# Third layer of an attention and two-MLP kernel: weight conversion pipelined over blocks, adding transfers in groups of six, first product block by block

## The chip, the cores and the metric

One NeuronCore of a Trainium2 chip runs the whole program. The metric is the device time of one execution in microseconds (us); of three runs of the kernel before, the median is 631.76 us (631.39 to 633.15). A change of under about 0.3% (1.9 us) can't be told from none.

The engines are TensorE (PE, with its weight loads PEld), VectorE (DVE), ScalarE (ACT) and GpSimd (POOL). Each works through its own queue in order, and so does SyncE (SP), which issues most transfers. POOL issues the transfers that add.

## The reference, cut to what matters

```
attn_out = attention(q, k, v)          # 2 batches, 8 heads, 768 x 64, banded mask
x = attn_out as 1536 x 512
a, b = x @ moe_w1, x @ moe_w2          # first MLP, d_ff 1024
x = ((a * b) @ moe_w3) @ moe_w_out
a, b = x @ moe2_w_a, x @ moe2_w_b      # second MLP, d_ff 1536
out = (a * b) @ moe2_w_out             # 1536 x 1536 times 1536 x 512: the third layer below
```

The weights are float64 and reach the chip as pairs of 32-bit words; q, k, v and the result are float32.

## The kernel before, in words

The change lies in the last 150 us: in the end of `products` and in `output`. Three things have to be known.

**Weights.** A block of 128 rows of `moe2_w_out` (blocks f = 0 to 11) is loaded as raw words by `wo_load` (L1013, queue SP) and turned into float32 by `convert`: ACT takes the two words apart (L89, L90), DVE joins them in three steps (L94, L98, L102) into the tile `wof`, ACT rounds the value to a high part (L115), and DVE subtracts to get the low part (L119); both parts are the tile `wo2`, which the trace shows as `wo_band`. `wo_steps(f)` does this for one block from first to last step; `fill` lets it advance between the products of PE.

**Products.** Every product of high and low parts is three matmuls (`multiply`, L931). `output` has two stages. The first is a plain product for the last 512 rows of the output: twelve blocks f of 12 matmuls 128x512, three into each of four PSUM banks. For each pair of blocks the left side is split into its parts by `rest_steps` (ACT L1028, DVE L1030). After block 11, ACT copies the four banks out (L1209).

The second stage computes the other 1024 rows with seven products of half-size matrices in place of eight, in the order 1, 2, 7, 6, 4, 5, 3. Each product is 72 matmuls 128x256 into four banks (rows i = 0 to 3), over six blocks f. The generator `prepare` makes the operands; one of its stages is run (`next(turns)`) ahead of each product, so what it puts into the queues of ACT and DVE stands ahead of that product's own evictions (ACT L1240, DVE L1243). An operand of the left side is made by `left`: a cast on ACT (L733), a subtraction on DVE (L734). There are eight PSUM banks: products 1 and 2 fill four each, and product 7 takes over the four of product 2 when DVE has evicted them (L1243).

**Adding transfers.** `add` (L1126) is a transfer issued from POOL that adds one 128x512 tile to another in SBUF. There are four sums for each f = 0 to 5, called S1 to S4 here: S1 is `ga[f][:,0] += ga[f][:,1]`, S2 `ga[f][:,1] += ga[f+6][:,1]`, S3 `ga[f][:,0] += ga[f+6][:,1]`, S4 `ga[f+6][:,0] += ga[f][:,0]`. S1 may start when the operand of product 1 for this f has been made (`first_left`), since it overwrites its source; S2 has to wait for S1 of the same f, which reads what S2 writes. Product 7 reads the sums S1, product 6 S3, product 5 S2 and product 3 S4.

The order of the work is that in which the Python code emits it; each engine's queue keeps that order, and an engine waits at an instruction whose semaphore has not come.

Of the kernel before, what the change touches and what calls it, by code (L numbers as in the profile page):

```python
# [9 lines left out]
F32R = mybir.dt.float32r  # L10
# [6 lines left out]
P = 128  # L17
# [14 lines left out]
class Emitter:  # L32
# [981 lines left out]

    def wo_steps(self, f):
        if f % 2 == 0:
            self.wo_whole[f // 2] = self.unit("wof", [P, 2, self.DM])
        t = self.unit("wo2", [P, 2, 1, self.DM], F32R)
        g = self.wo_whole[f // 2][:, f % 2 : f % 2 + 1]
        for stage in self.convert(t[:, 0], t[:, 1], self.wo_raw.pop(f), g):  # L1020
            for _ in stage():
                yield
        self.wo[f] = t

# [14 lines left out]
    def products(self, ops, tail):  # L1039


        nc, C, nf2 = self.nc, self.C, self.NF2
        H = TG // 2
# [3 lines left out]
        self.ga, self.gb = ga, gb  # L1047
        self.wo_raw, self.wo, self.wo_whole, self.rests = {}, {}, {}, {}
        order0 = [(0, 1), (0, 7), (0, 2), (0, 6), (0, 4), (1, 1), (1, 7), (0, 5), (1, 6), (1, 4), (1, 2), (1, 5), (0, 3), (1, 3)]
        order = [(0, 1), (0, 7), (1, 1), (1, 7), (0, 6), (0, 4), (1, 6), (1, 4), (0, 5), (1, 5), (0, 2), (1, 2), (0, 3), (1, 3)]  # L1050
# [4 lines left out]
        for f in range(nf2):  # L1055
# [10 lines left out]
            for slot, (q, k) in enumerate(order if f else order0):  # L1066
# [5 lines left out]
                if f == nf2 - 1:  # L1072
                    if slot in (0, 2, 4):
                        self.wo_load(slot // 2)
                    if slot == 2:
                        steps += [self.wo_steps(0), self.rest_steps(0), self.wo_steps(1), self.wo_steps(2)]
                    if slot > 2:
                        self.fill(steps)
                for _ in range(1 if f else 0 if slot < 3 else 1 if slot < 8 else 2):
# [39 lines left out]
    def output(self):  # L1119
# [34 lines left out]
        def first_left(f):  # L1154
            left(1, f, ga[f][:, 0])
            add(ga[f][:, 0], ga[f][:, 1])
            add(ga[f][:, 1], ga[f + K][:, 1])

        def prepare():
            lefts(2, lambda f: ga[f + K][:, 0])  # L1160
            for j in range(K // 2):
                b, d = whole[j], whole[j + K // 2]
                t3 = self.half("t3", [P, 2, H])
                sub(t3, d[:, :, high], b[:, :, high])
                right(7, t3)
            yield
            lefts(7, lambda f: ga[f][:, 0], lambda f: add(ga[f][:, 0], ga[f + K][:, 1]))
            for j in range(K // 2):
                b, d = whole[j], whole[j + K // 2]
                sub(b[:, :, low], b[:, :, high], b[:, :, low])  # L1170
                sub(b[:, :, high], d[:, :, high], b[:, :, low])
            yield
            for j in range(K // 2):
                right(6, whole[j][:, :, high], -1.0)
            lefts(6, lambda f: ga[f][:, 0], lambda f: add(ga[f + K][:, 0], ga[f][:, 0]))
            yield
            for j in range(K // 2):
                b, d = whole[j], whole[j + K // 2]
                sub(d[:, :, low], d[:, :, low], b[:, :, high])
                right(4, d[:, :, low], -1.0)  # L1180
            lefts(4, lambda f: ga[f + K][:, 1])
            yield
            for j in range(K // 2):
                right(5, whole[j][:, :, low], -1.0)
            lefts(5, lambda f: ga[f][:, 1])
            yield
            lefts(3, lambda f: ga[f + K][:, 0])
            yield
            yield

        banks = [self.bank("o") for _ in range(4)]
        for f in range(nf2):
            if f + 3 < nf2:
                self.wo_load(f + 3)
            steps = []
            if f + 3 < nf2:
                steps.append(self.wo_steps(f + 3))
            if f % 2 == 0 and f + 2 < nf2:
                steps.append(self.rest_steps(f // 2 + 1))
            hi, lo = self.rests[f // 2]  # L1200
            for n, p in enumerate(banks):
                at = slice(n * P, (n + 1) * P)
                left_part = hi[:, f % 2, at], lo[:, f % 2, at]
                self.multiply(p, [left_part], [(wo[f][:, 0, 0], wo[f][:, 1, 0])], f == 0, f == nf2 - 1)
                for _ in range(3):
                    self.fill(steps)
# [5 lines left out]
            for step in steps:  # L1212
                for _ in step:
                    pass
            for e in {8: (0,), 9: (1, 2), 10: (3, 4), 11: (5,)}.get(f, ()):
                first_left(e)
# [7 lines left out]
        turns = prepare()  # L1224
        z, x, m = [None] * 4, [None] * 4, [None] * 4
        sums = {}
        for k in (1, 2, 7, 6, 4, 5, 3):
            next(turns)
            for i in range(4):
                if k in (1, 2, 7):  # L1230
                    {1: z, 2: x, 7: m}[k][i] = self.bank("o", (P, H))
                bank = {2: x, 7: m, 4: m}.get(k, z)[i]
                h, e = divmod(i, 2)
                at = slice(i * P, (i + 1) * P)
                terms = [(t[:, 0, at], t[:, 1, at]) for t in la[k]]
                self.multiply(bank, terms, rb[k], k in (1, 2, 7), True, k in (6, 4, 5, 3))
                if k in (1, 7, 6, 3) and e == 0:
# [140 lines left out]
```

## Time and profile before

| | |
|---|---|
| median of 3 runs | 631.76 us |
| profiled execution: device time, span | 631.91 us, 630.0 us |
| TensorE busy | 588.9 us, 93% |
| VectorE, ScalarE, GpSimd busy | 452.5 us, 364.3 us, 156.2 us |
| granted clock, mean | 0.98 |
| first matmul of `output` | 500.09 us |
| first matmul of product 7 | 579.92 us |

Busy time of TensorE over the whole span hides where it waits: up to 500 us it is busy nearly without a break, and its idle time after that lies in the two stages of `output`. Times in the rows below are us from the start of the span, so they are to be compared with the 630.0 us and not with the 631.91 us.

### The profile page before, as it was taken

How to read it: one execution, taken by the hardware profiler on the slowest of the kernel's cores; microseconds unless marked ns; L12 is line 12 of the kernel's file. 1: busy time of each engine (PE TensorE's matmuls, PEld its weight loads, DVE VectorE, ACT ScalarE, POOL GpSimd, SP SyncE). 2: the span in 40 equal slices, each digit the busy share in tenths (PEclk: the TensorE clock that was granted, in tenths of full speed). 3: DMA queues.
4: the chain of work that ended last, by engine and by line, in shares of the span. 5: the costliest groups of instructions: out<-in, count | busy, mean ns of one | idle time of the engine just before them, and what ended most of it. 6: DMA issues, size and time to landing. Idle time of an engine off the chain costs nothing.

```text
span 630.0 us, 10247 instructions
## 1 busy us (share of the span) xinstructions
PE 588.9 (93%) x3632; PEld 511.6 (81%) x3632; DVE 452.5 (72%) x978; ACT 364.3 (58%) x796; POOL 156.2 (25%) x214
## 2 busy tenths in 40 slices
PE   6998999999999999999999999999999978881996
PEld 4677978888888888888999888888888856781996
DVE  6888899369774855489996777777776877645680
ACT  6998899656473746387544444454444555732450
POOL 5655766200000003216120222222222000136200
PEclk9999999999999999999999999999999988995999
DMA  8999762344242325967131221201221630457911
GB/s 239 268 254 211 194 175 71 137 135 164 89 170 74 133 68 105 227 137 107 27 134 34 68 82 56 80 17 68 68 67 63 206 100 33 111 92 130 172 48 59
DMA packets 28556, 73.63 MB, mean 117 GB/s; under 512 B 3408, under 2 KB 8016, under 8 KB 28496
## 3 DMA queue, kind: packets, MB, share of 16 engines
q1 hardware_dynamic: 20560, 57.42, 30.7%
q0 software_dynamic: 7360, 14.68, 13.6%
q10 hardware_dynamic: 576, 0.79, 0.5%
q8 instruction: 30, 0.49, 0.3%
q14 instruction: 30, 0.25, 0.1%
HBM read 55.05 MB, written 3.15 MB: 92 GB/s over the span
## 4 chain that ended last, share of the span: by engine, by line
PE 74%; DVE 11%; DMA 6%; ACT 5%; issue 3%; POOL 1%; POOLq 0%; DVEq 0%; ACTq 0%
PE ab_band L931 26%; PE y_band L931 9%; PE o_band L931 7%; PE ab_band L669 6%; PE ab_band L670 6%; PE ab_band L671 6%; DMA ga_band<-ga_band 4%; PE wfp_band L245 2%; PE wfp_band L244 2%; PE wfp_band L243 2%; PE pv_band L516 2%; PE pt_band L480 2%; DVE s_band L444 1%; DVE wof_band L102 1%; DVE wof_band L98 1%
## 5 line engine op out<-in xcount | busy, mean ns | idle before, releaser
L931 PE MATMUL ab_band<-y_band,ws_band 128*128 128x512 f32 (+1 forms) x576 | 110.2, 337 | 0.0
L931 PEld LDWEIGHTS ab_band<-y_band,ws_band 128*128 128x128 f32 x576 | 90.9, 190 | 12.2 <-ACT u_band L1085 0.2
L669 PE MATMUL ab_band<-xh_band,w_band 128*128 128x512 f32 (+1 forms) x216 | 81.8, 379 | 0.0
L671 PE MATMUL ab_band<-xh_band,w_band 128*128 128x512 f32 (+1 forms) x216 | 79.0, 366 | 0.0
L670 PE MATMUL ab_band<-xl_band,w_band 128*128 128x512 f32 (+1 forms) x216 | 79.0, 366 | 0.0
L931 PE MATMUL o_band<-wo_band,gs_band 128*128 128x256 f32 (+1 forms) x360 | 63.9, 339 | 9.2 <-DVE gs_band L1030 9.1
L469 POOL TENSOR_SCALAR s_band<-s_band,z_band 128x256 f32<-128x256 f32 (+1 forms) x96 | 61.1, 649 | 35.8 <-DVE z_band L467 15.5
L931 PEld LDWEIGHTS o_band<-wo_band,gs_band 128*128 128x128 f32 x360 | 55.1, 197 | 18.0 <-DVE gs_band L1030 11.2
L931 PE MATMUL y_band<-gs_band,wf_band 128*128 128x512 f32 (+1 forms) x336 | 58.4, 336 | 0.0
L931 PEld LDWEIGHTS y_band<-gs_band,wf_band 128*128 128x128 f32 x336 | 51.8, 190 | 6.6
L931 PE MATMUL ab_band<-y_band,wa_band 128*128 128x512 f32 (+1 forms) x288 | 56.4, 338 | 0.0
L90 ACT ACTIVATE raw_band<-raw_band 128x512 int32<-128x512 uint32 x76 | 51.1, 673 | 0.0
L931 PE MATMUL o_band<-wt_band,gs_band 128*128 128x256 f32 x288 | 36.7, 292 | 15.4 <-DVE s_band L1243 15.4
L931 PEld LDWEIGHTS ab_band<-y_band,wa_band 128*128 128x128 f32 x288 | 46.0, 190 | 6.1
L678 DVE TENSOR_TENSOR g_band<-ab_band,b_band 128x512 f32<-128x512 f32 (+1 forms) x27 | 16.9, 629 | 45.2 <-ACT b_band L677 45.2
L931 PEld LDWEIGHTS o_band<-wt_band,gs_band 128*128 128x128 f32 x288 | 36.5, 202 | 15.6 <-issue 15.6
L456 ACT ACTIVATE s_band<-s_band,m_band 128x256 f32<-128x256 f32 (+1 forms) x96 | 47.0, 499 | 3.5 <-DVE m_band L444 3.4
L669 PEld LDWEIGHTS ab_band<-xh_band,w_band 128*128 128x128 f32 x216 | 40.7, 188 | 7.5 <-issue 1.0
L671 PEld LDWEIGHTS ab_band<-xh_band,w_band 128*128 128x128 f32 x216 | 40.6, 188 | 6.7
L670 PEld LDWEIGHTS ab_band<-xl_band,w_band 128*128 128x128 f32 x216 | 40.7, 189 | 6.2
L1085 ACT COPY p_band<-ab_band 128x512 f32<-128x512 f32 (+1 forms) x48 | 21.9, 482 | 36.8 <-PE ab_band L931 36.8
L1126 POOL DMA_DIRECT2D ga_band<-ga_band x24 | 20.9, 1273 | 85.8 <-DVE gs_band L734 59.3
(149 smaller groups left out, 1205.3 us busy)
## 6 DMA issues: line engine op xcount, KB each, us to landing
raw_band<-in_moe_w_dram SPq DMA_DIRECT2D x31, 512.0 KB, 4.7
raw_band<-in_moe_w_out_dram SPq DMA_DIRECT2D x20, 512.0 KB, 3.6
raw_band<-in_moe_w_b_dram SPq DMA_DIRECT2D x12, 512.0 KB, 3.5
raw_band<-in_moe_w_a_dram SPq DMA_DIRECT2D x12, 512.0 KB, 4.4
ga_band<-ga_band POOLq DMA_DIRECT2D x24, 256.0 KB, 5.5
v_band<-in_v_dram SPq DMA_DIRECT2D x12, 256.0 KB, 8.1
kd_band<-in_kq_dram SPq DMA_DIRECT2D x12, 256.0 KB, 7.9
qd_band<-in_kq_dram SPq DMA_DIRECT2D x12, 256.0 KB, 7.9
```

What stands on the lines that cost most here:

```text
L90: nc.scalar.activation(out=low, in_=low.bitcast(U32), func=AF.Copy, scale=2.0**-29)
L243: nc.tensor.matmul(acc, w[:, 1, k % 4, :], o[:, 0, 0, :], start=(k == 0), stop=False)
L244: nc.tensor.matmul(acc, w[:, 0, k % 4, :], o[:, 1, 0, :], start=False, stop=False)
L456: nc.scalar.activation(out=s[:, j, lo:], in_=s[:, j, lo:], func=AF.Exp, bias=m[:, j : j + 1], scale=-1.0, accum_out=z[:, j : j + 1],)
L469: nc.gpsimd.tensor_scalar(out=s[:, j, lo:], in0=s[:, j, lo:], scalar1=z[:, j : j + 1], scalar2=1.0, op0=ALU.mult, op1=ALU.mult)
L669: nc.tensor.matmul(p, wl, xh, start=(c == 0), stop=False)
L670: nc.tensor.matmul(p, wh, xl, start=False, stop=False)
L671: nc.tensor.matmul(p, wh, xh, start=False, stop=(c == self.C - 1))
L678: nc.vector.tensor_tensor(out=out[:, at], in0=ps[0], in1=b, op=ALU.mult)
L931: self.nc.tensor.matmul(bank, wt, xt, start=start and i == n == 0, stop=stop and n == 2 and i == len(terms) - 1, skip_group_check=more,)
L1085: copy = lambda out: nc.scalar.copy(out=out, in_=bank)
L1126: add = lambda out, a: nc.gpsimd.dma_start(out, a, accum_op=ALU.add)
```

## The change

`wo_steps` becomes one generator over all twelve blocks: while block f is joined and rounded, block f+1 has been taken apart, and the low part of block f-1 is subtracted after the rounding of f. In the last block of `products` four raw blocks are loaded in place of three, and nine steps of the new generator are run; in `output`, `wo_until` runs it as far as a block needs, with a lead of three blocks, and blocks are loaded five ahead in place of three. `first_left` issues S1 only; f = 0 to 3 are emitted in the first stage, 4 and 5 in `prepare`. The sums S2 follow as a group behind the sums S3, and the sums S4 as a group behind the six operands of product 6. Product 1 runs block by block over its four banks in place of bank by bank.

```diff
-    def wo_steps(self, f):
...
+    def wo_steps(self):
+        stages = {}
+
+        def begin(f):
+            if f % 2 == 0:
+                self.wo_whole[f // 2] = self.unit("wof", [P, 2, self.DM])
+            g = self.wo_whole[f // 2][:, f % 2 : f % 2 + 1]
+            self.wo[f] = t = self.unit("wo2", [P, 2, 1, self.DM], F32R)
+            stages[f] = self.convert(t[:, 0], t[:, 1], self.wo_raw.pop(f), g)
+            for _ in stages[f].pop(0)():
+                pass
+
+        begin(0)
+        yield
+        for f in range(self.NF2 + 1):
+            if f + 1 < self.NF2:
+                begin(f + 1)
+            if f < self.NF2:
+                for stage in stages[f][:2]:
+                    for _ in stage():
+                        yield
+            if f:
+                for _ in stages.pop(f - 1)[2]():
+                    pass
+                self.wo_done = f
                 yield
-        self.wo[f] = t
+
+    def wo_until(self, f):
+        while self.wo_done < f:
+            next(self.wo_turns)
...
+        self.wo_done, self.wo_turns = 0, self.wo_steps()
...
-                    if slot in (0, 2, 4):
+                    if slot in (0, 2, 4, 6):
                         self.wo_load(slot // 2)
-                    if slot == 2:
-                        steps += [self.wo_steps(0), self.rest_steps(0), self.wo_steps(1), self.wo_steps(2)]
-                    if slot > 2:
-                        self.fill(steps)
+                    if slot == 5:
+                        steps.append(self.rest_steps(0))
+                    if slot > 4:
+                        next(self.wo_turns)
...
             add(ga[f][:, 0], ga[f][:, 1])
-            add(ga[f][:, 1], ga[f + K][:, 1])
 
         def prepare():
+            for f in (4, 5):
+                first_left(f)
             lefts(2, lambda f: ga[f + K][:, 0])
...
             lefts(7, lambda f: ga[f][:, 0], lambda f: add(ga[f][:, 0], ga[f + K][:, 1]))
+            for f in range(K):
+                add(ga[f][:, 1], ga[f + K][:, 1])
...
-            lefts(6, lambda f: ga[f][:, 0], lambda f: add(ga[f + K][:, 0], ga[f][:, 0]))
+            lefts(6, lambda f: ga[f][:, 0])
+            for f in range(K):
+                add(ga[f + K][:, 0], ga[f][:, 0])
...
+            self.wo_until(f + 1)
+            target = min(f + 3, nf2)
...
-                for _ in range(3):
+                if self.wo_done < target:
+                    next(self.wo_turns)
+                if n % 2:
                     self.fill(steps)
...
-            for e in {8: (0,), 9: (1, 2), 10: (3, 4), 11: (5,)}.get(f, ()):
+            self.wo_until(target)
+            for e in {10: (0, 1), 11: (2, 3)}.get(f, ()):
                 first_left(e)
...
+            if k == 1:
+                z = [self.bank("o", (P, H)) for _ in range(4)]
+                for f in range(K):
+                    for i, bank in enumerate(z):
+                        at = slice(i * P, (i + 1) * P)
+                        t = la[1][f]
+                        self.multiply(bank, [(t[:, 0, at], t[:, 1, at])], [rb[1][f]], f == 0, f == K - 1)
```

VectorE's queue in the first stage of `output`. Before, around blocks 6 and 7 (`wo_band_5670` and `wo_band_5692`), with the split of the next left side (L1030) behind:

```order
L98 SCALAR_TENSOR_TENSOR wof_band_5669<-raw_band_5664,wof_band_5669 128x512
L102 ISA wof_band_5669<-raw_band_5664,wof_band_5669 128x1024
L119 TENSOR_TENSOR wo_band_5670<-wof_band_5669,wo_band_5670 128x512
L94 TENSOR_SCALAR wof_band_5669<-wof_band_5669 128x512
L98 SCALAR_TENSOR_TENSOR wof_band_5669<-raw_band_5687,wof_band_5669 128x512
L102 ISA wof_band_5669<-raw_band_5687,wof_band_5669 128x1024
L119 TENSOR_TENSOR wo_band_5692<-wof_band_5669,wo_band_5692 128x512
L1030 TENSOR_TENSOR gs_band_5707<-gb_band_4704,gs_band_5706 128x1024
```

After the change, the same place: blocks 6, 7 and 8 are `wo_band_5650`, `wo_band_5676` and `wo_band_5699`.

```order
L102 ISA wof_band_5649<-raw_band_5644,wof_band_5649 128x1024
L1051 TENSOR_TENSOR gs_band_5708<-gb_band_4704,gs_band_5707 128x1024
L119 TENSOR_TENSOR wo_band_5650<-wof_band_5649,wo_band_5650 128x512
L94 TENSOR_SCALAR wof_band_5698<-wof_band_5698 128x512
L98 SCALAR_TENSOR_TENSOR wof_band_5698<-raw_band_5671,wof_band_5698 128x512
L102 ISA wof_band_5698<-raw_band_5671,wof_band_5698 128x1024
L119 TENSOR_TENSOR wo_band_5676<-wof_band_5649,wo_band_5676 128x512
```

The low part L119 of a block now stands behind the join (L94, L98, L102) of the next block, and no longer right behind its own.

GpSimd's queue of adding transfers, from the first one on (`ga_band_3829` is f = 0, then 3972, 4118, 4264, 4410 and 4557; `ga_band_4703` to `ga_band_5432` are f + 6). Before:

```order
L1126 DMA ga_band_3829<-ga_band_3829 128x512
L1126 DMA ga_band_3829<-ga_band_4703 128x512
L1126 DMA ga_band_3972<-ga_band_3972 128x512
L1126 DMA ga_band_3972<-ga_band_4850 128x512
L1126 DMA ga_band_4118<-ga_band_4118 128x512
L1126 DMA ga_band_4118<-ga_band_4996 128x512
```

After the change:

```order
L1148 DMA ga_band_3829<-ga_band_3829 128x512
L1148 DMA ga_band_3972<-ga_band_3972 128x512
L1148 DMA ga_band_4118<-ga_band_4118 128x512
L1148 DMA ga_band_4264<-ga_band_4264 128x512
L1148 DMA ga_band_4410<-ga_band_4410 128x512
L1148 DMA ga_band_4557<-ga_band_4557 128x512
L1148 DMA ga_band_3829<-ga_band_4703 128x512
```

The six sums S1 now follow each other, and the sums S2 no longer stand between them.

ScalarE's queue at the end of the first stage. Before, the casts for f = 0 to 4, the copies of the four banks, then the cast for f = 5:

```order
L733 CAST gs_band_5811<-ga_band_3829 128x512
L733 CAST gs_band_5828<-ga_band_3972 128x512
L733 CAST gs_band_5833<-ga_band_4118 128x512
L733 CAST gs_band_5850<-ga_band_4264 128x512
L733 CAST gs_band_5855<-ga_band_4410 128x512
L1209 COPY o_band_5863<-o_band_5585 128x512
L1209 COPY o_band_5869<-o_band_5586 128x512
L1209 COPY o_band_5875<-o_band_5587 128x512
L1209 COPY o_band_5881<-o_band_5588 128x512
L733 CAST gs_band_5884<-ga_band_4557 128x512
```

After the change:

```order
L733 CAST gs_band_5835<-ga_band_3829 128x512
L733 CAST gs_band_5839<-ga_band_3972 128x512
L1238 COPY o_band_5846<-o_band_5580 128x512
L1238 COPY o_band_5852<-o_band_5581 128x512
L1238 COPY o_band_5858<-o_band_5582 128x512
L1238 COPY o_band_5864<-o_band_5583 128x512
L733 CAST gs_band_5867<-ga_band_4118 128x512
L733 CAST gs_band_5871<-ga_band_4264 128x512
```

Four of the six casts for product 1 now stand behind the copies, which wait for the end of block 11.

## Rows read from the trace of the kernel before

**Rows 1.** Waits, 495 to 630 us: waiter, releaser, us in total, times, longest.
```profile
POOL ga_band L1126 <- DMA ga_band<-ga_band: 25.7, 9, 4.6
PE o_band L931 <- DVE s_band L1243: 15.4, 1, 15.4
```
**Rows 2.** Timeline of TensorE: start, us, instruction, count, idle before it.
```profile
500.09 5.63 PE L931 MATMUL o_band<-wo_band,gs_band 128*128 128x512 f32 x24
508.72 7.37 PE L931 MATMUL o_band<-wo_band,gs_band 128*128 128x512 f32 x24 [3.00 <-DVE gs_band L1030]
...
541.09 23.40 PE L931 MATMUL o_band<-wo_band,gs_band 128*128 128x512 f32 x168 [2.35 <-DVE gs_band L1030]
```
**Rows 3.** Timeline of VectorE, same columns.
```profile
492.84 0.68 DVE L1086 TENSOR_TENSOR u_band<-ab_band,u_band 128x512 f32<-128x512 f32 x1
...
503.50 0.42 DVE L1107 TENSOR_TENSOR gb_band<-ab_band,p_band 128x256 f32<-128x256 f32 x1
...
508.58 0.42 DVE L94 TENSOR_SCALAR wof_band<-wof_band 128x512 int32<-128x512 int32 x1
509.03 0.69 DVE L98 SCALAR_TENSOR_TENSOR wof_band<-raw_band,wof_band 128x512 int32<-128x512 int32 x1
509.86 0.69 DVE L102 CUSTOM_DVE_ANT_0 wof_band<-raw_band,wof_band 128x1024 uint16<-128x1024 uint16 x1
511.29 0.69 DVE L119 TENSOR_TENSOR wo_band<-wof_band,wo_band 128x512 fp32r<-128x512 f32 x1 [0.74 <-ACT wo_band L115]
511.90 0.42 DVE L94 TENSOR_SCALAR wof_band<-wof_band 128x512 int32<-128x512 int32 x1
...
515.52 1.22 DVE L1030 TENSOR_TENSOR gs_band<-gb_band,gs_band 128x1024 fp32r<-128x1024 f32 x1 [0.26 <-ACT gs_band L1028]
516.66 0.42 DVE L94 TENSOR_SCALAR wof_band<-wof_band 128x512 int32<-128x512 int32 x1
...
548.01 4.30 DVE L734 TENSOR_TENSOR gs_band<-ga_band,gs_band 128x512 fp32r<-128x512 f32 x7 [3.96 <-ACT gs_band L733]
552.23 0.69 DVE L1146 TENSOR_TENSOR t_band<-wof_band,wof_band 128x512 f32<-128x512 f32 x1
...
559.20 1.90 DVE L734 TENSOR_TENSOR gs_band<-ga_band,gs_band 128x512 fp32r<-128x512 f32 x3 [0.91 <-ACT gs_band L733]
...
575.37 0.68 DVE L1146 TENSOR_TENSOR wof_band<-wof_band 128x512 f32<-128x512 f32 x1
...
579.36 1.41 DVE L1243 TENSOR_TENSOR s_band<-o_band,s_band 128x256 f32<-128x256 f32 x4
```
**Rows 4.** Timeline of ScalarE, same columns.
```profile
510.64 0.62 ACT L115 CAST wo_band<-wof_band 128x512 fp32r<-128x512 f32 x1 [2.11 <-DVE wof_band L102]
511.17 0.67 ACT L89 ACTIVATE wof_band<-raw_band 128x512 f32<-128x512 f32 x1
511.74 0.68 ACT L90 ACTIVATE raw_band<-raw_band 128x512 int32<-128x512 uint32 x1
...
514.44 1.05 ACT L1028 CAST gs_band<-gb_band 128x1024 fp32r<-128x1024 f32 x1
...
547.35 3.74 ACT L733 CAST gs_band<-ga_band 128x512 fp32r<-128x512 f32 x7
```
**Rows 5.** Timeline of GpSimd, same columns.
```profile
574.37 7.92 POOL L1126 DMA_DIRECT2D ga_band<-ga_band  x9 [3.38 <-DMA ga_band<-ga_band]
```
**Rows 6.** The chain that ended last: start, us, what.
```profile
541.94 4.06 DMA ga_band<-ga_band
...
579.92 45.35 PE o_band L931 x360
```
**Rows 7.** DMA queue of GpSimd: packets, MB, share of 16 engines over the span.
```profile
q0 software_dynamic: 7360, 14.68, 13.6%
```
**Rows 8.** Windows: length; PE, PEld, DVE, ACT, POOL busy (count); granted clock; DMA share; GB/s.
```profile
508.69:516.77 8.08, 7.37 (x24) 5.56 (x24) 6.05 (x10) 4.49 (x7) 0.00 (x0) 0.79 0.19 65
579.92:584.12 4.20, 4.20 (x20) 4.20 (x21) 4.20 (x9) 1.93 (x4) 3.23 (x4) 0.50 1.10 180
```

More of the change, by code (lines that the diff above doesn't have):

```diff
@@ L1013, in wo_load @@
         self.nc.sync.dma_start(self.wo_raw[f], self.io["moe2_w_out"][f].unsqueeze(1))
-    def wo_steps(self, f):
[L1016 to L1021, printed above, removed]
+    def wo_steps(self):
[21 more added lines that the diff above has]
+                self.wo_done = f
                 yield
-        self.wo[f] = t
+    def wo_until(self, f):
+        while self.wo_done < f:
+            next(self.wo_turns)
     def rest_steps(self, j):
@@ L1192, in output @@
         for f in range(nf2):
-            if f + 3 < nf2:
-                self.wo_load(f + 3)
+            for e in range(f + 5 if f else 4, min(f + 6, nf2)):
+                self.wo_load(e)
             steps = []
-            if f + 3 < nf2:
-                steps.append(self.wo_steps(f + 3))
             if f % 2 == 0 and f + 2 < nf2:
                 steps.append(self.rest_steps(f // 2 + 1))
+            self.wo_until(f + 1)
+            target = min(f + 3, nf2)
             hi, lo = self.rests[f // 2]
@@ L1224, in output @@
         turns = prepare()
-        z, x, m = [None] * 4, [None] * 4, [None] * 4
+        x, m = [None] * 4, [None] * 4
         sums = {}
@@ L1228, in output @@
             next(turns)
+            if k == 1:
[5 more added lines that the diff above has]
+                        self.multiply(bank, [(t[:, 0, at], t[:, 1, at])], [rb[1][f]], f == 0, f == K - 1)
             for i in range(4):
-                if k in (1, 2, 7):
-                    {1: z, 2: x, 7: m}[k][i] = self.bank("o", (P, H))
+                if k in (2, 7):
+                    {2: x, 7: m}[k][i] = self.bank("o", (P, H))
                 bank = {2: x, 7: m, 4: m}.get(k, z)[i]
@@ L1235, in output @@
                 terms = [(t[:, 0, at], t[:, 1, at]) for t in la[k]]
-                self.multiply(bank, terms, rb[k], k in (1, 2, 7), True, k in (6, 4, 5, 3))
+                if k != 1:
+                    self.multiply(bank, terms, rb[k], k in (2, 7), True, k in (6, 4, 5, 3))
                 if k in (1, 7, 6, 3) and e == 0:
```

## The prediction

> **What bounds the kernel now.** I read the page first, then the waits of the last 135 us, the timelines of the engines there, the chain that ended last, and windows for the clock. TensorE starts `output` at 500.09 us. It then waits in two ways. In the first stage it stops at five pairs of blocks, 3.00 us at the first and 2.35 at the last, released by the split of the next left side on VectorE [rows 2]. Between products 2 and 7 it stops once, for 15.4 us, released by the eviction L1243 [rows 1]. From 579.92 us on nothing stops it: 360 matmuls in one run of 45.35 us [rows 6].
>
> The first kind comes from the hand-over inside one conversion. VectorE ends the join L102, ScalarE rounds, and only then can L119 run: VectorE stands still for 0.74 us [rows 3], and there is another such hand-over before L1030 (0.26 us idle, after ScalarE's cast). A pair of blocks thus takes 8.08 us from one L1030 to the next, 508.58 to 516.66 with what follows them, while VectorE is busy for 6.05 of 8.08 us [rows 3, 8]. TensorE needs far less: 24 matmuls in 5.63 us, 5.46 without the drain of the last, 0.228 each [rows 2].
>
> The second kind is a queue. The eviction L1243, which frees a bank for product 7, stands on VectorE behind the six operands of product 7 and six subtractions. The operands wait for the sums S1, and GpSimd issues S1 and S2 in turn, each S2 waiting for its S1 to land: 25.7 us of waiting there [rows 1].
>
> **The change, step by step.** I follow one path: VectorE's first L119, its L119 of block 10, the end of block 11 on TensorE, the operands, the eviction, product 7.
>
> *Start.* Before, VectorE works without a real break from the eviction at 492.84 to 503.83 (start and length of L1107 at 503.50, 0.33 to the next start) [rows 3]. Afterwards the same stretch holds the same evictions and two joins, but no L119: two of 0.61 us less (511.29 to 511.90), and its start is not held up by an earlier L119, some 0.3 us. So the first L119 starts at 503.83 - 1.22 - 0.3 = 502.3. TensorE, at 500.09 + one matmul, waits for it until 503.0, 2.7 us. That is a new wait, right at the beginning; before, this block was finished long ahead. It is not lost for itself, since VectorE is the bound of what follows.
>
> *Conversion.* From start to start VectorE takes 0.45 for L94 and 0.83 for L98 [rows 3]; L102 I put at 0.60, as L119, an instruction of the same length. A join is 1.88, a low part 0.61, an L1030 1.14 (515.52 to 516.66). From the first L119 to that of block 10 stand ten L119 (6.1), ten joins (18.8) and five L1030 (5.7), 30.6 us. The rounding now has a whole join of time, so the 0.74 goes. What may be late next is ScalarE's cast for L1030: it stands behind L115 (0.53), L89 and L90 (0.57 each), so it starts 1.67 after the L115 and takes 1.05 [rows 4]: with the 0.78 from L102 to L115, VectorE may take the result 3.5 us after the start of that L102, and reaches its L1030 after 3.09. I charge 0.4 three times, 1.2 us; the ends are 0 and 10 x 0.74 = 7.4. L119 of block 10 starts at 502.3 + 31.8 = 534.1. A pair costs 6.1 to 6.5 us then, against 5.46 on TensorE: VectorE stays the bound and TensorE's slack hides a slow start of the clock, as after the wait of 3.00 us, when 24 matmuls took 7.37 at a mean granted clock of 0.79 [rows 2, 8].
>
> *End of the first stage.* 0.74 from the start of that L119 to its release, then 22 matmuls at 0.228: block 11 ends at 534.1 + 0.74 + 5.02 = 539.9. Before, 541.09 + 24 x 0.228 = 546.6. Gain 6.7.
>
> *Operands.* ScalarE's four copies now stand ahead of four casts of product 1. Before, the cast began 0.75 after the end of block 11 (547.35) and VectorE's L734 at 548.01, so it starts at 539.9 + 1.4 = 541.3. Ten of these in a row (four of product 1, six of product 2) at 0.61 give 6.1: 547.4. Product 1, block by block, needs the third operand only 24 matmuls after 539.9, 2.9 us later, so the moved casts are covered; if that cover were gone, product 1 would start late, but TensorE has 5 us of slack before product 7. Then as before from the first L1146 to the first operand of product 7, 552.23 to 559.20: 6.97, to 554.4.
>
> *Transfers.* S1 of f = 2 to 5 are issued from 542.3 on (the operand's 0.69 and some 0.3 after 541.3), 0.88 apart (nine in 7.92) [rows 5]. One alone lands after 4.06 [rows 6]. In a row each takes the 16 engines for 13.6% x 630.0 us x 0.262 / 14.68 = 1.53 us [rows 7]. The last lands near 542.3 + 4.1 + 3 x 1.53 = 551.0, and its cast comes only at 557: 6 us of cover. So the six operands run at VectorE's pace, 3.7 us, then the six subtractions as before (575.37 to 579.36, 3.99), to 562.0 for L1243, and 0.56 to product 7: 562.6. TensorE ends product 2 at 539.9 + 17.9 (23.40 - 5.46) = 557.8, so about 5 us of waiting remain of 15.4.
>
> *After product 7 starts.* S3 is issued from 555 on, S2 behind it, then S4: S3 has landed by 555 + 4.1 + 5 x 1.53 = 567, product 6 begins at 562.6 + 45.35 / 5 + 1.7 = 573. S2 lands 9.2 us later than S3, S4 18.4 later (586), products 5 and 3 begin at 591 and 600. All hidden. The tail keeps its 45.35 us, with the slow clock of its start: 0.50 for 4.2 us [rows 8], 2.1 us lost. After 5 us of waiting I keep the same 2.1; the ends are 0 and 2.1. The matmuls of product 1 are the same in number and form, only their banks alternate, as in the first stage: 0, bounded either way by what lies between 17.9 / 144 = 0.124 for one and half of the 0.228 there, 0.114: 72 x 0.01 = 0.7 us, which the 5 us cover.
>
> The sum: 579.92 - 562.6 = 17.3 us earlier. Against the profiled execution's own 631.91 us that is 614.6, and 0.15 less against the median of 631.76: 614.5 us.
>
> At the transfers a page speaks against the change. Rows first: nine issues took 7.92 us from 574.37 on, while VectorE ran L1146 and L1243 back to back from 575.37 to 580.8 [rows 3, 5], so none was held. The Trainium skill, "SBUF - State Buffer", section "SBUF: two separate sides", says that a VectorE instruction can hold the SBUF port pair with which GpSimd writes a transfer's descriptors, and that a transfer issued from GpSimd then waits. By the row the cost is nothing; by that rule it is the third rival below.
>
> **The rivals.**
>
> 1. *The conversion doesn't overlap.* L119 still waits its 0.74, through ScalarE's queue, which is in order and now holds the next block's L89 and L90 ahead. Then a pair keeps 8.08, L119 of block 10 comes at 502.3 + 5 x 8.08 = 542.7, and product 7 at 571.2: 623. For it: ScalarE's late cast above. Against: it is busy for only 4.49 of 8.08 us [rows 8].
>
> 2. *The sums stay serial.* Landing 4.06 plus about 1 for issue and semaphore each, one after the other, as before: S1 of f = 5 lands at 542.3 + 4 x 5.1 = 562.7, its operand takes 0.65 to its L734, then 0.61 + 3.99 + 0.56: product 7 at 568.5, 620.5. Against: each now waits for VectorE alone.
>
> 3. *GpSimd is held while VectorE runs.* Behind product 7's operands VectorE runs without a break through the subtractions, four L1243 and three low parts, to about 565.3. If S3 were issued only then, the last lands at 565.3 + 4.1 + 7.7 = 577, its operand is ready at 578.5, and product 6, which wants it at 575, waits 3.4 us: 618.
>
> 4. *Less waiting remains.* No late cast (1.2) and no slow clock at the start of product 7 (2.1): 611.2. With TensorE alone as the bound from 503 on, 50.8 us to the end of product 2, it would be 605.5; nothing in the order allows that.
>
> 5. *Slower: the clock stays low.* The waits become short and frequent, at the end of each pair. If the granted clock stayed at its lower level (0.50, 1.2 GHz) from 503 on, TensorE's 50.8 us would become 101.6, product 7 would start at 604.6, and the end comes 24.7 us later than before: 656. It turns slower once product 2 ends near 579, that is from 26 us of loss on the 50.8. The rows show a low clock after waits of 3.00 us and of 15.4, and none in the 23.40 us run after a wait of 2.35 [rows 2, 8]. The Trainium skill, "TensorE: Matmul & The Clock Gate", section "A second HAM failure mode: psum-queue depth-cycling", describes such a kernel: short idle times between groups of matmuls make the clock swing. The run after 2.35 us speaks against it here.
>
> **How the numbers follow.** Forecast with small errors in its terms (612.5 to 616.5): 0.58. Rival 4: 0.12. Rival 3: 0.10. Rival 2: 0.07. Rival 1: 0.07. Rival 5: 0.03. The change doing nothing that can be told, below 0.3% (1.9 us, about what a measurement of this kernel can tell from none): 0.03. The range of 8 in 10 is 610.5 to 620.0: it holds the forecast, rival 3, half of rival 2 and most of 4. Faster by over 0.3%: 0.94; within: 0.03; slower: 0.03.
>
> **What will show it.** In the profile of the changed kernel: a wait of TensorE of 2 to 3 us just after 500 us; VectorE busy for over 0.9 of the time from 503 to 534, L119 without idle time before it; pairs 6.1 to 6.5 us apart; block 11 ending near 540; GpSimd's waits for its own transfers mostly gone and S1 issued 0.9 us apart; one wait of some 5 us before product 7 near 562, released by L1281 (the old L1243); no wait after. It is wrong if ScalarE's casts or the landing of a sum, not VectorE's queue, release the operands of product 7, or if TensorE waits at product 6.

## The result and the profile after

The changed kernel takes 614.87 us (614.65 to 615.85, 4 runs) against 631.66 (631.39 to 633.15), a ratio of 0.9732 with a 95% interval of 0.9714 to 0.9751: 16.8 us, 2.7%, faster. Five more runs of it, in the series of kernels 9 to 11 below, gave 614.17 us, 0.9712 [0.9689, 0.9736]. The profiled execution took 615.08 us, with a span of 613.3 against 630.0.

TensorE's timeline after the change (start, us, instruction, count, idle time before it and what ended it) answers to [rows 2]:

```profile
500.72 0.39 PE L931 MATMUL o_band<-wo_band,gs_band 128*128 128x512 f32 x1
503.21 18.15 PE L931 MATMUL o_band<-wo_band,gs_band 128*128 128x512 f32 x71 [2.10 <-DVE wo_band L119]
521.63 0.50 PE L931 MATMUL o_band<-wo_band,gs_band 128*128 128x512 f32 x1 [0.27 <-DVE gs_band L1051]
...
534.78 22.77 PE L931 MATMUL o_band<-wo_band,gs_band 128*128 128x512 f32 x167 [0.20 <-DVE wo_band L119]
562.62 37.28 PE L931 MATMUL o_band<-wt_band,gs_band 128*128 128x256 f32 x288 [5.07 <-DVE s_band L1281]
```

The five stops between pairs (3.00, 0.71, 2.36, 0.71 and 2.35 us before) are gone. One stop of 2.10 us stands at the start instead, then only some of 0.2 to 0.3, and 5.07 of the 15.43 us before product 7. VectorE's timeline in the same form shows why, beside [rows 3]:

```profile
502.48 0.68 DVE L119 TENSOR_TENSOR wo_band<-wof_band,wo_band 128x512 fp32r<-128x512 f32 x1
...
510.38 0.69 DVE L102 CUSTOM_DVE_ANT_0 wof_band<-raw_band,wof_band 128x1024 uint16<-128x1024 uint16 x1
510.99 0.69 DVE L119 TENSOR_TENSOR wo_band<-wof_band,wo_band 128x512 fp32r<-128x512 f32 x1
511.59 0.42 DVE L94 TENSOR_SCALAR wof_band<-wof_band 128x512 int32<-128x512 int32 x1
...
513.89 1.23 DVE L1051 TENSOR_TENSOR gs_band<-gb_band,gs_band 128x1024 fp32r<-128x1024 f32 x1 [0.32 <-ACT gs_band L1049]
...
533.95 1.29 DVE L119 TENSOR_TENSOR wo_band<-wof_band,wo_band 128x512 fp32r<-128x512 f32 x2
...
541.46 6.11 DVE L734 TENSOR_TENSOR gs_band<-ga_band,gs_band 128x512 fp32r<-128x512 f32 x10 [5.02 <-ACT gs_band L733]
...
554.45 3.71 DVE L734 TENSOR_TENSOR gs_band<-ga_band,gs_band 128x512 fp32r<-128x512 f32 x6 [0.90 <-ACT gs_band L733]
...
562.06 1.41 DVE L1281 TENSOR_TENSOR s_band<-o_band,s_band 128x256 f32<-128x256 f32 x4
```

L119 follows L102 after 0.61 us, from start to start, without idle time; it belongs to the block before. In the conversion only the cast for L1051 still comes late, by 0.32 us. The line at 541.46 holds the next loss: VectorE stands still for 5.02 us there. GpSimd's timeline, and the waits from 495 us on (waiter, releaser, us in total, times, longest), which answer to [rows 1, 5]:

```profile
542.45 3.51 POOL L1148 DMA_DIRECT2D ga_band<-ga_band  x4 [4.53 <-DVE gs_band L734]
555.44 11.46 POOL L1148 DMA_DIRECT2D ga_band<-ga_band  x13 [9.49 <-DVE gs_band L734]
```
```profile
PE o_band L931 <- DVE s_band L1281: 5.1, 1, 5.1
...
POOL ga_band L1148 <- DMA ga_band<-ga_band: 3.0, 3, 1.2
```

Thirteen issues in a row take 11.46 us, 0.88 each, while VectorE works without a break, and GpSimd's waits for its own transfers fall from 25.7 to 3.0 us. The windows (columns as in [rows 8]):

```profile
502.90:534.00 31.10, 29.89 (x119) 23.18 (x119) 28.83 (x46) 20.71 (x34) 0.00 (x0) 0.95 0.18 62
562.80:567.00 4.20, 4.20 (x20) 4.20 (x21) 4.20 (x10) 3.01 (x7) 4.10 (x5) 0.50 1.10 179
```

VectorE is busy for 28.83 of 31.10 us, 93%; before it was 6.05 of 8.08, 75% [rows 8].

### The profile page after: what moved, and what is told of

Same layout as the page of the kernel before. It is cut to its first block, busy times and chain, and to the rows that moved or that the text cites. A ratio compares the mean times of both kernels' runs of the same rounds, so it can differ in the third digit from the quotient of the medians.

```text
span 613.3 us, 10259 instructions
## 1 busy us (share of the span) xinstructions
PE 587.6 (96%) x3632; PEld 510.9 (83%) x3632; DVE 450.7 (73%) x978; ACT 364.1 (59%) x796; POOL 156.2 (25%) x214
## 4 chain that ended last, share of the span: by engine, by line
PE 74%; DVE 10%; DMA 7%; ACT 4%; issue 3%; SPq 1%; DVEq 0%; ACTq 0%
PE ab_band L931 28%; PE y_band L931 9%; PE o_band L931 8%; PE ab_band L669 6%; PE ab_band L671 6%; PE ab_band L670 6%; DMA qd_band<-in_kq_dram 3%; PE wfp_band L243 2%; PE wfp_band L245 2%; PE wfp_band L244 2%; DMA kq_band<-in_kq_dram 2%; PE pv_band L516 2%; DMA raw_band<-in_moe_w_dram 1%; DMA v_band<-in_v_dram 1%; DVE s_band L444 1%
## 5 line engine op out<-in xcount | busy, mean ns | idle before, releaser
L931 PE MATMUL o_band<-wo_band,gs_band 128*128 128x256 f32 (+1 forms) x360 | 62.4, 334 | 3.2 <-DVE wo_band L119 2.7
L1108 DVE TENSOR_TENSOR u_band<-ab_band,u_band 128x512 f32<-128x512 f32 (+1 forms) x24 | 13.3, 555 | 38.1 <-PE ab_band L931 38.1
```

The lines of the kernel that those rows point to most:

```text
L931: self.nc.tensor.matmul(bank, wt, xt, start=start and i == n == 0, stop=stop and n == 2 and i == len(terms) - 1, skip_group_check=more,)
L1108: plus = lambda t: nc.vector.tensor_tensor(out=t, in0=bank, in1=t, op=ALU.add)
```

## The experiments

Each ran in 4 or 5 executions, one of them profiled. The start of `output` lies between 499.2 and 501.3 us in these profiles, for reasons that lie mostly ahead of the edits, so stages are compared by the distance from there to the start of product 7, both read from TensorE's timeline. What lies behind the start of product 7 is not in the distance. Each ratio is to the kernel before in the same series, whose medians lie between 631.66 and 632.31 us:

| kernel | `output` | product 7 | distance | median, us | ratio to before [95%] |
|---|---|---|---|---|---|
| before | 500.09 | 579.92 | 79.83 | 631.66 | |
| the change | 500.72 | 562.62 | 61.90 | 614.87 | 0.9732 [0.9714, 0.9751] |
| the change again | 500.19 | 562.09 | 61.90 | 614.17 | 0.9712 [0.9689, 0.9736] |
| 1 conversion alone | 501.26 | 573.98 | 72.72 | 626.05 | 0.9910 [0.9891, 0.9928] |
| 2 transfers alone | 499.97 | 569.05 | 69.08 | 623.86 | 0.9880 [0.9863, 0.9897] |
| 3 product 1 by bank | 500.14 | 562.04 | 61.90 | 614.16 | 0.9729 [0.9711, 0.9747] |
| 4 S2 behind each S1 | 501.03 | 573.21 | 72.18 | 624.97 | 0.9899 [0.9882, 0.9917] |
| 5 subtractions later | 501.25 | 559.16 | 57.91 | 610.92 | 0.9657 [0.9632, 0.9682] |
| 6 turns two steps earlier | 499.46 | 560.19 | 60.73 | 612.22 | 0.9688 [0.9667, 0.9709] |
| 7 low parts on GpSimd | 499.68 | 565.97 | 66.29 | 618.68 | 0.9791 [0.9768, 0.9814] |
| 8 = 5 and 7 | 499.68 | 562.00 | 62.32 | 615.16 | 0.9733 [0.9713, 0.9753] |
| 9 = 5 and 6 | 499.21 | 555.95 | 56.74 | 608.54 | 0.9626 [0.9602, 0.9650] |
| 10 six operands at block 10 | 500.05 | 559.52 | 59.47 | 610.45 | 0.9663 [0.9636, 0.9690] |
| 11 = 5, 6 and 10 | 500.87 | 556.32 | 55.45 | 606.68 | 0.9588 [0.9565, 0.9612] |

The changed kernel was run again beside 9 to 11: 

> The changed kernel once more, beside the three variants: 614.9 us by its first runs (614.65 to 615.85).

**1, 2: each half of the change alone.** In 1 the pipeline of the conversion stays, and transfers, first operands and product 1 are as before:

```diff
         def first_left(f):
             left(1, f, ga[f][:, 0])
             add(ga[f][:, 0], ga[f][:, 1])
+            add(ga[f][:, 1], ga[f + K][:, 1])
...
-            for e in {10: (0, 1), 11: (2, 3)}.get(f, ()):
+            for e in {8: (0,), 9: (1, 2), 10: (3, 4), 11: (5,)}.get(f, ()):
```

> Only the pipelined conversion of the changed kernel; the adding transfers, the first operands and product 1 stand as before. Theory (two separate waits, each released by its own chain): block 11 ends near 540 as in the changed kernel, but S1 and S2 in turn still take 32.15 us from the first issue (then 541.94, now some 6.4 earlier, after L119 of block 10) to the last landing of S1, so product 7 starts near 573.5 and the time is 625.5. Rival (the changed kernel's gain is the conversion, and the transfers only follow it): product 7 near 563, 615 to 617.

2 is the kernel before with exactly those parts of the change that 1 lacks (the diff above with its signs turned, S4 in its own loop, product 1 block by block).

> Only the grouped transfers, the moved first operands and product 1 block by block; the conversion runs one block from first to last step, as before. Theory: block 11 ends at 546.6 as before, from there the same 22.7 us to product 7 as forecast for the changed kernel: 569.3, 621.2 us, and TensorE waits 4.8 us before product 7. The two parts then add up (6.4 and 10.6 of 16.9 us). Rival (conversion and transfers overlap, so one alone gives most): under 618.

Measured: 626.05 and 623.86 us. Waits of kernel 1 from 500 us on, then two lines of TensorE's timeline of kernel 2:

```profile
POOL ga_band L1148 <- DMA ga_band<-ga_band: 25.6, 9, 5.2
...
PE o_band L931 <- DVE s_band L1268: 15.5, 1, 15.5
```
```profile
540.97 23.00 PE L931 MATMUL o_band<-wo_band,gs_band 128*128 128x512 f32 x168 [2.33 <-DVE gs_band L1030]
569.05 36.94 PE L931 MATMUL o_band<-wt_band,gs_band 128*128 128x256 f32 x288 [5.07 <-DVE s_band L1256]
```

Each half removes its own wait and leaves the other whole: 1 keeps the 15.5 us before product 7, 2 keeps the 2.33 us before the last pair and has the 5.07 of the whole change. By distance 1 is worth 79.83 - 72.72 = 7.1 us and 2 is worth 10.75; together 17.9, which is the change's 79.83 - 61.90. By time they give 5.7 and 7.8 of 16.8, less than the whole. In the profile of 1, `output` starts 1.2 us later than before. Of the four executions of 2 only the profiled one took the expected 621.2 us; the other three took 623.84 to 623.95, 2.7 more, at a lower mean granted clock (0.980 to 0.986 against 0.988). Where in them the clock was low, no profile shows.

**3: product 1 bank by bank again**, all else as changed:

```diff
-            if k == 1:
-                z = [self.bank("o", (P, H)) for _ in range(4)]
-                for f in range(K):
-                    for i, bank in enumerate(z):
...
-                if k in (2, 7):
+                if k in (1, 2, 7):
```

> The changed kernel with product 1 bank by bank again. Theory: the first bank now waits for the operand of f = 5, which VectorE ends at 544.0; product 1 and 2 end 1.9 us later, at 559.5, still ahead of the bank that VectorE frees at 562.5: no change, 614.9 within 0.5, and the wait before product 7 shrinks from 5.1 to 3.2 us. Rival (block by block is worth what it saves on TensorE): 616.8.

```profile
541.62 17.54 PE L931 MATMUL o_band<-wo_band,gs_band 128*128 128x256 f32 x138 [1.21 <-DVE gs_band L734]
562.04 34.79 PE L931 MATMUL o_band<-wt_band,gs_band 128*128 128x256 f32 x288 [2.88 <-DVE s_band L1273]
```

TensorE's timeline: it now waits 1.21 us in product 1 and 2.88 before product 7. The distance stays at 61.90, and the ratio is that of the change. This part of the change only moves waiting from one place to another, since VectorE's queue sets product 7. The profiled execution took 611.95 us and the other three 613.75 to 614.65; the last section has its clock.

**4: S2 back behind each S1**, all else as changed:

```diff
             add(ga[f][:, 0], ga[f][:, 1])
+            add(ga[f][:, 1], ga[f + K][:, 1])
...
-            for f in range(K):
-                add(ga[f][:, 1], ga[f + K][:, 1])
```

> The changed kernel with one thing undone: each sum S2 again stands right behind its S1 in GpSimd's queue. Theory: S1 of f = 0 is issued at 536.1 and S1 of f = 5 lands 32.15 later, at 568.3; 5.8 us on from there product 7 starts, at 574.1: 626.4 us, 11.5 over the changed kernel. Rival (the transfers would be hidden, VectorE's queue alone sets product 7): 615.

GpSimd's timeline, two of five such pairs of issues:

```profile
546.41 1.74 POOL L1148 DMA_DIRECT2D ga_band<-ga_band  x2 [4.60 <-DMA ga_band<-ga_band]
551.52 1.74 POOL L1148 DMA_DIRECT2D ga_band<-ga_band  x2 [3.37 <-DMA ga_band<-ga_band]
```

The issues are 5 to 6 us apart again instead of 0.88. The one edit takes back 72.18 - 61.90 = 10.3 of the 10.8 us of the transfers' half: independent transfers in a row are that half.

**5: the six subtractions of the weights** (L1168) behind product 2's evictions:

```diff
             for f in range(K):
                 add(ga[f][:, 1], ga[f + K][:, 1])
+            yield
             for j in range(K // 2):
                 b, d = whole[j], whole[j + K // 2]
                 sub(b[:, :, low], b[:, :, high], b[:, :, low])
                 sub(b[:, :, high], d[:, :, high], b[:, :, low])
-            yield
```

> The changed kernel with the six subtractions L1168 moved behind the evictions of product 2 in VectorE's queue. Theory (VectorE's queue is the last thing ahead of product 7): the eviction starts at 558.2, right behind the last operand of product 7, and product 7 at 558.7 in place of 562.6: 611.0 us; 609 if the clock doesn't fall after the shorter wait of about 1 us. Rival (the operands of product 6, which come 4 us later on VectorE, become the bound): what is gained at product 7 is waited for at product 6, 615.

```profile
559.16 10.66 PE L931 MATMUL o_band<-wt_band,gs_band 128*128 128x256 f32 x87 [1.09 <-DVE s_band L1281]
570.36 25.50 PE L931 MATMUL o_band<-wt_band,gs_band 128*128 128x256 f32 x201 [0.54 <-DVE gs_band L734]
```

610.92 us. Product 7 comes 3.99 us earlier by distance, to the hundredth what the six take in the forecast (575.37 to 579.36 in [rows 3]). So these 3.99 us of the wait were VectorE's queue, not ScalarE and not a landing.

That the time met the expected 611.0 is in part luck. The 611.0 counted on a slow clock behind the wait, and 609 on none. In the profile the clock stayed at 1.00 behind the wait of 1.09 us, and still this execution took 611.55 us. `output` starts 0.53 us later in it than in the change, and most of what the clock gave back was lost at product 6, with a new wait of 0.54 us (the place that the rival named), and in product 4 behind it (columns as in [rows 8]):

```profile
577.16:579.16 2.00, 2.00 (x14) 1.52 (x13) 2.00 (x4) 2.00 (x6) 0.00 (x0) 1.00 1.12 187
```

TensorE did 14 matmuls in these 2.00 us and 14 in the next, against 19 in the 2.00 us before, at a granted clock of 1.00. Its weight loads wait four times 0.19 us for L734 there: the operands of product 4 come at VectorE's pace. From the start of product 7 to the last matmul are 45.34 us, 1.92 more than in kernel 10 (43.42).

**6: the weight's turns from two steps earlier** in the stage before, so that TensorE finds the first L119 done:

```diff
-                    if slot > 4:
+                    if slot > 2:
                         next(self.wo_turns)
```

> The changed kernel with the generator started two slots earlier in the last block of products (eleven steps in place of nine), so that the first L119 is ahead of output. Theory (VectorE, not the wait of TensorE at 501 us, bounds the first stage): the wait of 2.1 us goes, but only the L94 and L98 that now fall into VectorE's idle time ahead of 493 shorten the path, 0.9 us: 614.0. Rival (the wait at the start is on the path): 612.8 or less.

```profile
499.46 0.39 PE L931 MATMUL o_band<-wo_band,gs_band 128*128 128x512 f32 x1
500.00 3.02 PE L931 MATMUL o_band<-wo_band,gs_band 128*128 128x512 f32 x12 [0.15 <-DVE wo_band L119]
503.30 3.02 PE L931 MATMUL o_band<-wo_band,gs_band 128*128 128x512 f32 x12 [0.28 <-DVE wo_band L119]
```

612.22 us, below the theory's 614.0 and within the rival's 612.8 or less. The distance speaks for the theory: 60.73 against 61.90 gives 1.17 us, near its 0.9, and of the wait of 2.10 us only this much was on the path. The rest of the 2.65 us between the medians is not explained by the stage: 1.26 us are the earlier start of `output` in this profile, which other kernels with the old turns show as well (7 and 8, 499.68), and against the second series of the change the ratios differ by only 0.0024, 1.5 us.

**7, 8: the low parts on GpSimd.** The five L1051 in this stage, 6.1 us of VectorE's 28.8, go to an engine that idles there:

```diff
-        self.nc.vector.tensor_tensor(out=lo, in0=src, in1=f32(hi), op=ALU.subtract)
+        engine = self.nc.gpsimd if j else self.nc.vector
+        engine.tensor_tensor(out=lo, in0=src, in1=f32(hi), op=ALU.subtract)
```

> The changed kernel with the low parts L1051 of the left side from pair 1 on done by GpSimd, which is idle there. Theory (VectorE bounds the first stage at 6.45 us a pair): without L1051 VectorE takes 5.0 a pair, TensorE's 5.46 becomes the bound, block 11 ends near 536.1 in place of 540.3 and the time is 611. An instruction takes GpSimd some 3 us, estimated as four times the 0.74 us of its L766 on a quarter of the elements. Rival (GpSimd's work on SBUF holds VectorE, as the Trainium skill has it in "SBUF - State Buffer", section "Who interferes with whom"): VectorE loses up to 3 us a pair, 620 or more.

8 has the edit of 5 as well. 

> The changed kernel with both: subtractions behind the evictions of product 2, and L1051 on GpSimd. Theory: the two gains stand one behind the other on the same path and add up, 3.9 + 3.8: 607.3. Rival (GpSimd holds VectorE): no better than with the subtractions moved alone, 611 or more.

Measured: 618.68 and 615.16 us, slower by 4.4 us of distance each time (66.29 - 61.90, 62.32 - 57.91). The theory that VectorE gains what it gives away is wrong. GpSimd's timeline of kernel 7, then VectorE's, then one line of TensorE's:

```profile
503.39 2.87 POOL L1052 TENSOR_TENSOR gs_band<-kq,gs_band 128x1024 fp32r<-128x1024 f32 x1 [21.37 <-ACT gs_band L1049]
514.07 2.46 POOL L1052 TENSOR_TENSOR gs_band<-gb_band,gs_band 128x1024 fp32r<-128x1024 f32 x1 [7.80 <-ACT gs_band L1049]
```
```profile
503.93 2.88 DVE L119 TENSOR_TENSOR wo_band<-wof_band,wo_band 128x512 fp32r<-128x512 f32 x1
...
511.71 0.42 DVE L94 TENSOR_SCALAR wof_band<-wof_band 128x512 int32<-128x512 int32 x1
...
513.61 0.69 DVE L119 TENSOR_TENSOR wo_band<-wof_band,wo_band 128x512 fp32r<-128x512 f32 x1
514.21 2.60 DVE L94 TENSOR_SCALAR wof_band<-wof_band 128x512 int32<-128x512 int32 x1
```
```profile
516.58 5.76 PE L931 MATMUL o_band<-wo_band,gs_band 128*128 128x512 f32 x24 [1.48 <-POOL gs_band L1052]
```

The L94 that starts 0.14 us behind GpSimd's instruction takes 2.60 us instead of 0.42 and ends 0.28 after it (516.81 against 516.53). The same happens at the other four: an L119 of 2.88 instead of 0.69, two more L94 of 2.60, an L102 of 2.89. VectorE is held for 2.2 us each time, 11 in all, more than the 6.1 of work taken from it. TensorE also waits for GpSimd's own results, three times 1.41 to 1.48 us, but the chain that ended last runs through the held instructions of VectorE and not through L1052. The Trainium skill, "SBUF - State Buffer", section "Who interferes with whom", says that GpSimd and VectorE share one pair of ports, that a VectorE instruction with two inputs in SBUF contends for it with a GpSimd instruction that reads SBUF, and that the one that comes second is blocked until the first is done. The trace agrees for the two-input forms (L119, L102); the one-input L94 was held as well, which the page gives for forms in a two-port mode, and no run here shows in which mode L94 ran.

**9: 5 and 6 together.** 

> The changed kernel with both edits that gained alone: the six subtractions behind product 2's evictions, and the weight turns of the stage before begun two steps earlier. Theory (the two lie on one path, VectorE's queue, and each moves product 7 by its own amount): the second moved block 10 by 1.2 us against the start of the output, the first left 1.09 of 5.07 us of waiting; 610.9 - 1.2 = 609.7 us, with a wait before product 7 still near 1.1 us. Rival (with product 7 no longer waiting, TensorE alone is the bound, and only half of the second edit counts): 610.4 us.

608.54 us, below both, and 5.63 below the change in the same series. The distances add exactly: 61.90 - 3.99 - 1.17 = 56.74, 5.16 less than the change; the other 0.5 us is not explained. Two pieces of the chain that ended last, from the part around product 6 (start, us, what):

```profile
555.77 9.86 DMA ga_band<-ga_band
...
567.13 34.16 PE o_band L931 x273
```

A 0.51 us wait at product 6 now goes back to an S3 that takes 9.86 us from issue to landing.

**10: all six operands of product 1 behind block 10.**

```diff
-            for e in {10: (0, 1), 11: (2, 3)}.get(f, ()):
+            for e in {10: (0, 1, 2, 3, 4, 5)}.get(f, ()):
...
         def prepare():
-            for f in (4, 5):
-                first_left(f)
```

> The changed kernel with all six operands of product 1 split behind block 10 of the first stage, none behind block 11 or later. Theory (VectorE stands still for 5.02 us there only because ScalarE's casts are queued behind the four evictions of block 11, so work put ahead of them is free): four of the ten L734 leave the queue behind block 11, 4 x 0.61 = 2.4 us, product 7 starts 2.4 us earlier after a wait of 2.6, 612.4 us. Rival (the buffers of those operands come free only when block 11 ends, so VectorE waits for them and nothing is won): 614.9 us or above.

VectorE's timeline, then TensorE's:

```profile
534.48 3.69 DVE L734 TENSOR_TENSOR gs_band<-ga_band,gs_band 128x512 fp32r<-128x512 f32 x6
540.78 3.70 DVE L734 TENSOR_TENSOR gs_band<-ga_band,gs_band 128x512 fp32r<-128x512 f32 x6 [2.60 <-ACT gs_band L733]
```
```profile
559.52 34.78 PE L931 MATMUL o_band<-wt_band,gs_band 128*128 128x256 f32 x288 [2.65 <-DVE s_band L1279]
```

610.45 us against 612.4: VectorE's idle time falls from 5.02 to 2.60, product 7 comes 2.43 us earlier (2.4 was expected), with 2.65 us of waiting (2.6 expected). Against the change in the same series the median falls by 3.72, 1.3 more than the distance. In the profile a gain beyond the distance is the clock: the 288 matmuls take 34.78 us at a granted clock of 1.00, against 37.28 and 36.53 in the two profiles of the change.

**11: all three**, the fastest version. 

> All three edits together: subtractions later, weight turns two steps earlier, six operands of product 1 behind block 10. Theory (VectorE's queue, then TensorE): the queue before product 7 is 2.4 us shorter than in the kernel with the first two, more than the 1.1 us of waiting left there, so TensorE runs without a wait from the first stage into product 7: 609.7 - 1.1 = 608.6 us. Rival (product 6's operands, which waited 0.54 us for L734 behind the moved subtractions, take over as the wait): 609.5 us.

The last piece of its chain:

```profile
533.75 66.80 PE o_band L931 x527
```

606.68 us, 0.9588 of before, 7.5 us below the change in the same series and 1.9 below the theory's 608.6. No idle time stands on TensorE from block 10 to the end; the three edits would give 7.59 us by distance and give 6.45, since TensorE is now the bound up to product 7. Neither the wait before product 7 nor that at product 6 is left. Another 0.94 us comes behind the start of product 7, where no slow clock stands now: 44.23 us to the last matmul, against 45.17 in the second profile of the change. Kernel 10 needs only 43.42, and the difference is again product 4:

```profile
574.32:576.32 2.00, 2.00 (x12) 1.41 (x11) 1.79 (x3) 2.00 (x7) 0.00 (x0) 1.00 1.12 195
```

Twelve matmuls in 2.00 us at a granted clock of 1.00, against 19 just before, while the weight loads wait three times 0.18 to 0.19 us for L734. So the next thing to shorten is the operands of product 4 on VectorE.

## Why the prediction was right

The forecast was 614.5 us, and the range 610.5 to 620.0. Its steps against the trace:

- *Start.* Forecast: first L119 at 502.3, 2.2 after the start of `output`, and 2.7 us of waiting. Measured: 502.48, which is 1.76 after it, and 2.10. Kernel 6 shows that the wait is real but only 1.17 us of it on the path. That TensorE's slack hides a slow clock there is shown: behind this wait the clock fell to 0.50 in the first profile of the change and stayed at 1.00 in the second (last section), and the distance is 61.90 us in both.
- *Conversion.* The 0.74 us per block are gone. The late cast, charged with three times 0.4, came three times with 0.31 to 0.34. Pairs take 6.46, 6.43 and 6.03 us from one L1051 to the next (6.1 to 6.5). L119 of block 10 starts at 533.95 (534.1).
- *End of the first stage.* 534.78 + 5.52 = 540.30 (539.9). It was 23 matmuls at 0.24 us, where 22 at 0.228 were counted.
- *Operands.* L734 resumes at 541.46 (541.3) and ends, with the next L1168, at 547.49 (547.4). The moved casts were covered: no wait stands in the 167 matmuls from 534.78 on. Without block order, in kernel 3, 1.21 us of waiting appears, and TensorE's slack before product 7 takes it.
- *Transfers.* First operand of product 7 at 554.45 (554.4), eviction at 562.06 (562.0), product 7 at 562.62 (562.6), 5.07 us of waiting (about 5). That VectorE's queue releases it, kernel 5 shows. Yet one sign that the prediction named for being wrong did occur: ScalarE's cast releases the first operand of product 7, 0.90 us late. It cost the sum nothing, since the kernel before has 0.91 at the same place and the 6.97 was carried over with it.
- *Tail.* 599.74 + 8.80 - 562.62 = 45.92 us, forecast 45.35. The slow clock was kept, as forecast, but for longer than the 4.2 us of the kernel before (columns as in [rows 8]):

```profile
566.62:568.62 2.00, 2.00 (x12) 2.00 (x12) 2.00 (x4) 0.89 (x2) 1.14 (x2) 0.58 1.10 201
```

  This is 4.00 to 6.00 us behind the start of product 7; in the kernel before the same stretch has a granted clock of 0.91. The price was taken as 2.1 us. Against the 34.78 us of kernel 10 without a slow clock, the 288 matmuls behind the wait take 37.28 us here, 2.5 more; 36.70 before, 1.9 more; and 36.53 in the second profile of the change, 1.75 more. So the price is not one number, and the longer tail is this term.

The sum thus came out by small errors of both signs: the path from the start of `output` to product 7 is 61.90 us where 562.6 - 500.09 = 62.5 was forecast (the start and the casts), `output` itself began 0.63 us later, and the tail is 0.58 longer. The span fell by 16.7 us; the forecast was 17.3. That the median is within 0.4 us of the forecast is in part luck, for each of these three is some 0.6 us and they do not have one sign; the mechanism holds step by step.

The rivals: that the conversion does not overlap and that the sums stay serial is refuted by the rows above (no idle time before L119; four of the sums S1 issued in 3.51 us). Kernel 2 shows what the first would have cost, 623.86 us against the 623 forecast. Kernels 1 and 4 show serial sums with S2 in between: 10.3 us of distance in kernel 4, where rival 2, without S2, was priced at 5.9. That GpSimd is held while VectorE runs is refuted for its issues: the 11.46 us of 13 issues lie beside L734, L1168, L1281 and L1162. The page cited there, the Trainium skill's "SBUF - State Buffer", says this of VectorE's two-port modes, in the section "SBUF: two separate sides" itself; the prediction left that condition out. Its section "Who interferes with whom" adds that a probe saw `tensor_copy` stall transfers and `tensor_tensor` not. With that the trace agrees for L734, L1168 and L1281, which are `tensor_tensor`. Kernel 7 shows the hold in the other direction, for GpSimd's arithmetic, of which the prediction says nothing. That less waiting remains did not happen, but kernels 5, 10 and 11 reach it by shortening VectorE's queue (its 605.5 is 605.7 by its own terms, 614.5 less 562.6 - 553.8); the forecast's remark that nothing in the order allows TensorE to be the bound holds for the change and not for 11. That the clock stays low is refuted: from 508 to 534 us it is 1.00 in both profiles of the change, with stops of 0.2 to 0.3 us at the pairs; the 0.95 from 502.9 to 534 is a single fall behind the first wait. The swing that the Trainium skill describes ("TensorE: Matmul & The Clock Gate", section "A second HAM failure mode: psum-queue depth-cycling") does not show here. But the prediction argued too much from the one run after 2.35 us. An equal wait two pairs earlier in the same trace did bring the low clock (TensorE's timeline, then a window):

```profile
524.93 7.38 PE L931 MATMUL o_band<-wo_band,gs_band 128*128 128x512 f32 x24 [2.36 <-DVE gs_band L1030]
```
```profile
526.00:530.00 4.00, 4.00 (x12) 3.17 (x11) 3.07 (x5) 1.78 (x3) 0.00 (x0) 0.57 0.00 0
```

## What to carry to other kernels

Where one engine's queue sets a path, add up that queue from its first instruction to the one that releases the wait; each instruction that can stand behind the releasing one is worth its full length, until the next engine is the bound. Independent transfers belong in a row on their queue, ahead of those that depend on them. An idle engine is no free place for work: GpSimd's arithmetic here took 2.2 us from VectorE for each 1.2 us that it took over.

## What the runs showed of the hardware

- VectorE is held by a GpSimd `tensor_tensor` that began before it: 2.60 us for an L94 of 0.42.
- The clock after a wait on TensorE is not one and the same. At the first wait of `output` the two profiles of the changed kernel differ, 2.10 us in the first and 2.14 in the second (windows of the first and of the second):

```profile
504.00:506.00 2.00, 2.00 (x6) 1.56 (x5) 1.86 (x3) 1.20 (x3) 0.00 (x0) 0.50 0.73 285
```
```profile
504.00:506.00 2.00, 1.74 (x8) 1.12 (x6) 2.00 (x3) 1.35 (x3) 0.00 (x0) 1.00 0.39 154
```

  So neither the kernel nor the length of the wait alone decides it. Ahead of product 7 it fell to 0.50 with waits of 5.07 us in the change, in its second profile and in kernels 2 and 6. In the profiles of kernels 3 and 10, behind waits of 2.88 and 2.65 us, it stayed at 1.00:

```profile
559.52:563.72 4.20, 4.20 (x35) 4.20 (x36) 4.20 (x9) 2.94 (x7) 4.20 (x5) 1.00 1.11 179
```

  This is kernel 10's window behind product 7's start (columns as in [rows 8]): 35 matmuls in 4.20 us, where the change has 20. Its five executions took 609.54, 609.79, 610.45, 612.05 and 612.07 us, at mean granted clocks of 0.996, 0.999, 0.993, 0.991 and 0.991: the two longest are 2.5 us above the shortest, as much as the slow clock cost in the tail of the change's first profile. That they lost it in this place is argued; only one execution was profiled. In kernel 10's profile the shortened wait did return more than its own length.
